# Transposing the normalised tile of a second MoE layer by VectorE and DRAM, in place of TensorE

## The chip, the cores and the metric

One core of a Trainium2 chip runs the whole program. The metric is the device time of one execution in microseconds (us). Engines: TensorE (PE; its weight loads are listed as PEld), VectorE (DVE), ScalarE (ACT), GpSimd (POOL) and SyncE (SP), whose queue issues most DMAs.

## What is computed

A Nystrom attention feeds two MoE layers. The change touches the second one, for 2304 tokens x, model width 512 and inner width 1024:

```python
def _moe2_ref(x, w_in, w_out, g_ln):
    h = x @ w_in
    e = np.exp(h - np.max(h, axis=-1, keepdims=True))
    sm = e / (np.sum(e, axis=-1, keepdims=True) + 1e-09)
    solu = h * sm
    mu = np.mean(solu, axis=-1, keepdims=True)
    var = np.mean((solu - mu) ** 2, axis=-1, keepdims=True)
    ln = (solu - mu) / np.sqrt(var + 1e-06) * g_ln
    return ln @ w_out
```

## The kernel before

The second layer is worked off in 18 tiles of 128 tokens, numbered 0 to 17, in the loop at L1001, after the first layer's last units. Numbers are split into a high half (copied into type fp32r by ACT) and a low half (the rest, subtracted by DVE), and a product takes three matmuls for each pair: high x high, high x low, low x high. In the traces the shapes say f32 for both.

One tile t passes these functions:

- `load_y` (L802) fetches the first layer's output from DRAM (yd) over SP's queue, `split_y` (L812) makes its halves (L127 on ACT, L128 on DVE).
- `gemm3` (L919), the first product: 24 matmuls of 512 columns into a PSUM tile h of two banks. There are two such tiles, so first product t waits until tile t-2's h has been read for the last time, by L940.
- `solu` (L930): the reduce to the row maximum (L935), the exponential (L937, ACT), the multiplication e * h (L940), the sum of squares (L943, ACT), an inverse square root by four Newton steps in short instructions (L953, L955) and the normalisation (L956), which writes a tile s of 128 tokens x 1024. It is a chain that goes from DVE to ACT and back twice.
- `lnT` (L959): the second product needs the 1024 inner columns on the partitions. TensorE transposes s in 8 blocks of 128 x 128 (L967) into two PSUM banks; ACT copies each bank into lh (L970), and DVE subtracts it into ll (L971).
- `gemm4` (L974), the second product: 24 matmuls of 512 columns, a copy out of PSUM by ACT (L983) and a store over SP's queue (L984).

The loop body at t calls, in this order, load_y(t+2), gemm3(t), solu(t), split_y(t+2), gemm4(t-3) and lnT(t-1). lh and ll have three buffers each, s and most others two. First product 0 runs before the loop, among the first layer's last matmuls.

Each engine and each DMA queue works its instructions off in a fixed order. A scheduler sets that order when the program is compiled: it goes by the order of the program text, but where an engine would stand in its own estimate it takes a later instruction that is ready. So an instruction of one tile can stand among those of another. The lines of the first layer that are mentioned: L612 and L623 (matmuls; L623 is the line of every product of three, named h or po by what it writes), L671 (the first layer's second product), L678 (its store to yd by ACT's queue), L222 and L231 (halves of weights), L468 (a transpose by DVE in blocks of 32 x 32).

Of the kernel before, what the change touches and what calls it, by code (L numbers as in the profile page):

```python
# [9 lines left out]
F32 = mybir.dt.float32  # L10
# [4 lines left out]
AF = mybir.ActivationFunctionType  # L15
ALU = mybir.AluOpType
# [6 lines left out]
def f(ap):  # L23
    return ap.bitcast(F32)
# [3 lines left out]
def nystrom_moe_kernel(  # L28
# [13 lines left out]
    V, A, PE, G, SP = nc.vector, nc.scalar, nc.tensor, nc.gpsimd, nc.sync  # L42
# [4 lines left out]
    P = 128  # L47
    L = 32
    R = S // L
    HG = 4  # L50
# [9 lines left out]
    NF2 = F2 // P  # L60
# [3 lines left out]
    NTT = NT // P  # L64
# [3 lines left out]
    PS = bass.MemoryType.PSUM  # L68

    const = ctx.enter_context(tc.tile_pool(name="const", bufs=1))  # L70
    dram = ctx.enter_context(tc.tile_pool(name="dram", bufs=1, space=bass.MemoryType.DRAM))
    yd = dram.tile([P, KD, NT], F32, name="yd")
    yp = dram.tile([P, KD, N], F32, name="yp")

    ident = const.tile([P, P], F32, name="ident")
    mask4 = const.tile([P, HG], F32, name="mask4")
# [603 lines left out]
    with ExitStack():  # L680
# [49 lines left out]
        for g in range(NG):  # L730
            prep, e, c, t, a = attn(0, g)
# [70 lines left out]
        def load_y(t):  # L802
            y = (tr if p2 is None else p2).tile([P, KD, P], F32, tag="y", name="y", bufs=1 if p2 is None else 2)
            SP.dma_start(out=y, in_=yd[:, :, t * P:(t + 1) * P])
            yt[t] = y
            n = min(N - t * P, P)
            if n > 0:
                z = tr.tile([P, KD, P], F32, tag="yz", name="yz")[:, :, 0:n]
                SP.dma_start(out=z, in_=yp[:, :, t * P:t * P + n])
                V.tensor_tensor(out=y[:, :, 0:n], in0=y[:, :, 0:n], in1=z, op=ALU.add)  # L810

        def split_y(t):  # L812
            src = yt[t]
            if t < 2:
                y2 = tr.tile([P, 2, KD, P], F32R, tag="yb", name="yb", bufs=2)
            else:
                y2 = p2.tile([P, 2, KD, P], F32R, tag="yb", name="yb")
            yh, yl = y2[:, 0], y2[:, 1]
            split(yh, yl, src)
            yt[t] = (yh, yl)  # L820
# [4 lines left out]
        for u, (s_, i) in enumerate(units):  # L825
            x = segs[s_][0] * CR // R, i // 4
# [21 lines left out]
        for p in range(U // 2):  # L848
            u = 2 * p + 1
            s_, i = units[u]  # L850
            c, i0, i1 = segs[s_]
# [65 lines left out]
        h2, ln, lt = {}, {}, {}  # L917

        def gemm3(t):  # L919
            yh, yl = yt.pop(t)  # L920
            h = ps_h2[t % len(ps_h2)].tile([P, 2, 512], F32, tag="h2", name="h2")
            for n in range(2):
                pairs = []
                for kk in range(KD):
                    vh, vl = (vi[n, kk // 2][:, kk % 2, x] for x in range(2))
                    pairs += [(yh[:, kk], vh), (yh[:, kk], vl), (yl[:, kk], vh)]
                mm3(h[:, n], pairs)
            h2[t] = h.rearrange("p a b -> p (a b)")
# [29 lines left out]

        def lnT(t):  # L959
            s = ln.pop(t)  # L960
            lh = p2.tile([P, NF2, P], F32R, tag="lh", name="lh", bufs=3)
            ll = p2.tile([P, NF2, P], F32R, tag="ll", name="ll", bufs=3)
            for j in range(2):
                pt = ps_t.tile([P, 512], F32, tag=f"t{j}", name="pt")
                for i in range(4):
                    c = 4 * j + i
                    PE.transpose(pt[:, i * P:(i + 1) * P], s[:, c * P:(c + 1) * P], ident)  # L967
                o = slice(4 * j, 4 * j + 4)
                ptv = pt.rearrange("p (c n) -> p c n", c=4)
                A.activation(out=lh[:, o], in_=ptv, func=AF.Copy)  # L970
                V.tensor_tensor(out=ll[:, o], in0=ptv, in1=f(lh[:, o]), op=ALU.subtract)  # L971
            lt[t] = (lh, ll)

        def gemm4(t):  # L974
            lh, ll = lt.pop(t)
            po = ps_o.tile([P, DM], F32, tag="o", name="po")
            pairs = []
            for c in range(NF2):
                vh, vl = (vo[c // 2][:, c % 2, x] for x in range(2))
                pairs += [(lh[:, c], vh), (lh[:, c], vl), (ll[:, c], vh)]  # L980
            mm3(po, pairs)
            ob = p2.tile([P, DM], F32, tag="ob", name="ob")
            A.activation(out=ob, in_=po, func=AF.Copy)  # L983
            SP.dma_start(out=out[t * P:(t + 1) * P, :], in_=ob)  # L984
# [10 lines left out]
        mo.close()  # L995
        p2 = ctx.enter_context(tc.tile_pool(name="p2", bufs=2, side="right"))
        ps_h2.append(ctx.enter_context(tc.tile_pool(name="ps_h2b", bufs=1, space=PS)))
        ps_t = ctx.enter_context(tc.tile_pool(name="ps_t", bufs=1, space=PS))
        ps_o = ctx.enter_context(tc.tile_pool(name="ps_o", bufs=2, space=PS))
        L4 = 3  # L1000
        for t in range(NTT + L4):  # L1001
            if t + 2 < NTT:
                load_y(t + 2)
            if t < NTT:
                if t:
                    gemm3(t)
                solu(t)
            if t + 2 < NTT:
                split_y(t + 2)
            for _ in range(3 if t < L4 else 100):  # L1010
                if w2 and next(w2[0], "end") == "end":
                    w2.pop(0)
            if t >= L4:
                gemm4(t - L4)
            if 1 <= t <= NTT:
                lnT(t - 1)


def _laid_out(name, a):
# [45 lines left out]
```

## Time and profile before

| | us |
|---|---|
| median of 3 runs | 663.92 |
| lowest and highest | 663.75, 666.64 |
| span of the profiled execution, first to last instruction | 663.1 |
| last matmul's end to the end of the span | 4.1 |
| PE busy | 629.6 (95%) |
| DVE busy | 386.2 (58%) |
| ACT busy | 313.6 (47%) |

For the profiled execution the record has the span; no time beside it is given. Busy shares are over the whole span, of which the second layer's stage takes the last third; rows of that stage, and of the chain of waits that ended last, say more about the change than the shares. A bracket behind a timeline row is the time that the engine was idle before the instruction, and what ended it. [...]

### The profile page before, as it was taken

What the parts mean: (1) busy time and instruction counts of PE and PEld (TensorE: products, weight loads), DVE (VectorE), ACT (ScalarE), POOL (GpSimd) and SP (SyncE); (2) the same over time, 40 slices, a digit from 0 to 9 for tenths busy, and PEclk for the clock granted to TensorE, in tenths of its full rate; (3) what the DMA queues carried; (4) which work ended last, traced back from release to release, by engine and by line L of the source; (5) the groups of instructions that cost most, each with busy time, mean ns of one, the idle gap of its engine ahead of it and who ended that gap; (6) DMA issues with size and microseconds to landing.
All of it is one profiled execution on the core that took longest, in us unless ns stands there. A gap on an engine that the chain in (4) does not pass through costs nothing.

```text
span 663.1 us, 11837 instructions
## 1 busy us (share of the span) xinstructions
PE 629.6 (95%) x4808; PEld 532.7 (80%) x4808; DVE 386.2 (58%) x976; ACT 313.6 (47%) x580; POOL 40.5 (6%) x21
## 2 busy tenths in 40 slices
PE   5688999999999999999997999999999999999997
PEld 2356877889889878898866998997888888888886
DVE  6899898932737235413537613456866666566560
ACT  2379985543637345434644524535534333343431
POOL 3420000000000000000014201310000000000000
PEclk9758899999999999999997999999999999999999
DMA  8998031310212010101055104223101111110001
GB/s 327 400 408 310 0 111 35 109 37 15 95 37 81 29 37 1 38 1 37 1 164 160 37 1 126 102 64 99 48 33 53 44 48 47 36 60 17 17 32 49
DMA packets 30583, 55.43 MB, mean 84 GB/s; under 512 B 3648, under 2 KB 19008, under 8 KB 30528
## 3 DMA queue, kind: packets, MB, share of 16 engines
q1 hardware_dynamic: 25344, 49.36, 21.3%
q10 hardware_dynamic: 5184, 5.31, 2.4%
q8 instruction: 38, 0.62, 0.4%
q14 instruction: 17, 0.14, 0.1%
HBM read 44.63 MB, written 10.03 MB: 82 GB/s over the span
## 4 chain that ended last, share of the span: by engine, by line
PE 87%; ACT 4%; DMA 3%; DVE 2%; issue 1%; POOL 1%; SPq 0%; ACTq 0%; POOLq 0%
PE y L671 30%; PE h L623 28%; PE po L623 15%; PE pa L612 3%; PE pt L967 2%; PE pa L298 2%; DMA r<-in_moe_w_in_dram 2%; PE pa L442 2%; PE pa L429 1%; PE pa L353 1%; POOL r L151 1%; DMA yd<-ye 1%; DMA scr_w<-in_k_dram 1%; DVE r L163 1%; PE pa L410 1%
## 5 line engine op out<-in xcount | busy, mean ns | idle before, releaser
L671 PE MATMUL y<-gh,hl 128*128 128x288 f32 x1024 | 161.7, 304 | 3.7 <-ACT ye L677 2.5
L671 PEld LDWEIGHTS y<-gh,hl 128*128 128x128 f32 x1024 | 144.5, 193 | 15.4 <-issue 7.4
L623 PE MATMUL h<-AT,u 128*128 128x288 f32 x768 | 124.7, 308 | 4.6 <-ACT s L648 2.2
L658 DVE TENSOR_TENSOR gl<-s,gh 128x288 fp32r<-128x288 f32 x128 | 55.0, 467 | 115.5 <-ACT gh L656 60.1
L623 PEld LDWEIGHTS h<-AT,u 128*128 128x128 f32 x768 | 109.8, 195 | 15.1 <-ACT u L615 4.2
L623 PE MATMUL h<-hl,yb 128*128 128x512 f32 x432 | 103.5, 394 | 1.3 <-DVE st L936 0.9
L623 PEld LDWEIGHTS h<-hl,yb 128*128 128x128 f32 x432 | 79.7, 188 | 18.0 <-DVE st L936 1.3
L623 PE MATMUL po<-hl,lh 128*128 128x512 f32 x288 | 88.8, 390 | 0.0
L671 PE MATMUL y<-gl,hl 128*128 128x288 f32 x512 | 83.2, 299 | 0.0
L656 ACT ACTIVATE gh<-s 128x288 fp32r<-128x288 f32 x128 | 50.7, 438 | 56.4 <-PE y L671 56.2
L671 PEld LDWEIGHTS y<-gl,hl 128*128 128x128 f32 x512 | 72.9, 190 | 4.2 <-issue 3.0
L648 ACT ACTIVATE s<-h 128x576 f32<-128x576 f32 x64 | 41.7, 651 | 69.5 <-PE h L623 66.0
L623 PEld LDWEIGHTS po<-hl,lh 128*128 128x128 f32 x288 | 53.9, 188 | 11.1
L623 PE MATMUL po<-hl,ll 128*128 128x512 f32 x144 | 56.1, 390 | 0.0
L151 POOL TENSOR_SCALAR r<-r 128x1024 f32<-128x1024 f32 x10 | 30.5, 3053 | 368.8 <-DMA r<-in_moe_w_in_dram 309.2
L943 ACT ACTIVATE e<-s,st 128x1024 f32<-128x1024 f32 x18 | 20.7, 1151 | 30.0 <-DVE st L942 29.8
L937 ACT ACTIVATE e<-h,st 128x1024 f32<-128x1024 f32 x18 | 20.1, 1117 | 31.2 <-DVE st L936 31.2
L935 DVE TENSOR_REDUCE st<-h 128x1 f32<-128x1024 f32 x18 | 22.0, 1223 | 20.1 <-PE h L623 15.2
L127 ACT ACTIVATE yb<-y 128x512 fp32r<-128x512 f32 x18 | 11.3, 631 | 46.6 <-PE h L623 45.7
L612 PE MATMUL pa<-w,W 64*32 64x512 f32 x256 | 28.1, 642 | 5.1 <-DVE u L616 4.0
L623 PEld LDWEIGHTS po<-hl,ll 128*128 128x128 f32 x144 | 27.0, 188 | 5.6
L616 DVE TENSOR_TENSOR u<-pa,u 128x512 fp32r<-128x512 f32 x32 | 21.1, 687 | 13.9 <-ACT u L615 13.5
(168 smaller groups left out, 678.0 us busy)
## 6 DMA issues: line engine op xcount, KB each, us to landing
r<-in_moe_w_in_dram SPq DMA_DIRECT2D x8, 1024.0 KB, 8.6
ro<-in_moe_w_out_dram SPq DMA_DIRECT2D x8, 1024.0 KB, 17.9
yd<-ye ACTq DMA_DIRECT2D x32, 144.0 KB, 1.8
y<-yd SPq DMA_DIRECT2D x18, 256.0 KB, 3.2
out_dram<-ob SPq DMA_DIRECT2D x18, 256.0 KB, 2.0
w<-in_moe_w_in_dram SPq DMA_DIRECT2D x4, 1024.0 KB, 10.5
v<-in_v_dram SPq DMA_DIRECT2D x8, 512.0 KB, 4.2
r<-in_moe_w_out_dram SPq DMA_DIRECT2D x4, 1024.0 KB, 4.9
```

The lines of the kernel that those rows point to most:

```text
L151: G.tensor_scalar(out=x, in0=x, scalar1=2.0 ** -112, scalar2=None, op0=ALU.mult)
L298: PE.matmul(out[r], lhsT=lhsT[r], rhs=rhs[r], start=True, stop=True)
L612: mm = PE.matmul(po[g][h * L:(h + 1) * L], lhsT=wb[b][r, g, h * L:(h + 1) * L], rhs=w[r, h], start=True, stop=True)
L616: V.tensor_tensor(out=u[:, 1, g], in0=po[g], in1=f(u[:, 0, g]), op=ALU.subtract))
L623: PE.matmul(o, lhsT=a, rhs=b_, start=i == 0, stop=i == n - 1)
L648: A.activation(out=s, in_=h, func=AF.Mish)
L656: A.activation(out=gh[:, e], in_=s[:, e], func=AF.Copy)
L658: V.tensor_tensor(out=gl[:, e], in0=s[:, e], in1=f(gh[:, e]), op=ALU.subtract)
L671: PE.matmul(yb[s_][d][:, 0:N], lhsT=w_out(s, i + e)[:, d * P:(d + 1) * P], rhs=r[:, e], start=i == i0 and e == k == 0, stop=i + 2 == i1 an ...
L935: V.tensor_reduce(out=st[:, 0:1], in_=h, op=ALU.max, axis=AX.X)
L937: A.activation(out=e, in_=h, func=AF.Exp, bias=st[:, 1:2], accum_out=st[:, 2:3])
L943: A.activation(out=e, in_=s, func=AF.Square, bias=st[:, 4:5], accum_out=st[:, 5:6])
```

## The change

`lnT` transposes s on DVE in blocks of 32 x 32, in one instruction for the tile, into a tile sT in SBUF. Four DMAs, one for each block of 32 partitions, write sT to one of three DRAM buffers (lnd), each with 1 KB runs; one DMA reads the buffer back, with the blocks where a full transposition has them, into lT in SBUF. All five are on SP's queue, and the read waits for the writes. A new function `split_ln` makes lh and ll out of lT, with one copy on ACT and one subtract on DVE, both over 1024 columns in SBUF; it is called one round of the loop later than the halves were made before, and still a round ahead of the second product. The two PSUM banks of `ps_t` are no longer used.

```diff
--- before.py
+++ after.py
@@ -71,6 +71,7 @@
     dram = ctx.enter_context(tc.tile_pool(name="dram", bufs=1, space=bass.MemoryType.DRAM))
     yd = dram.tile([P, KD, NT], F32, name="yd")
     yp = dram.tile([P, KD, N], F32, name="yp")
+    lnd = [dram.tile([HG, HG, L, NF2 * L], F32, name=f"lnd{i}") for i in range(3)]
 
     ident = const.tile([P, P], F32, name="ident")
     mask4 = const.tile([P, HG], F32, name="mask4")
@@ -958,17 +959,23 @@
 
         def lnT(t):
             s = ln.pop(t)
+            sT = p2.tile([P, HG, NF2, L], F32, tag="sT", name="sT")
+            V.transpose(out=sT, in_=s.rearrange("p (c q j) -> p q c j", q=HG, j=L))
+            z = lnd[t % len(lnd)]
+            for a in range(HG):
+                SP.dma_start(out=z[a].rearrange("q j x -> j q x"),
+                             in_=sT[a * L:(a + 1) * L].rearrange("j q c i -> j q (c i)"))
+            lT = p2.tile([P, HG, NF2, L], F32, tag="lT", name="lT")
+            SP.dma_start(out=lT.rearrange("p a c i -> p a (c i)"), in_=z.rearrange("a q j x -> (q j) a x"))
+            lt[t] = lT
+
+        def split_ln(t):
+            src = lt[t].rearrange("p a c i -> p c a i")
             lh = p2.tile([P, NF2, P], F32R, tag="lh", name="lh", bufs=3)
             ll = p2.tile([P, NF2, P], F32R, tag="ll", name="ll", bufs=3)
-            for j in range(2):
-                pt = ps_t.tile([P, 512], F32, tag=f"t{j}", name="pt")
-                for i in range(4):
-                    c = 4 * j + i
-                    PE.transpose(pt[:, i * P:(i + 1) * P], s[:, c * P:(c + 1) * P], ident)
-                o = slice(4 * j, 4 * j + 4)
-                ptv = pt.rearrange("p (c n) -> p c n", c=4)
-                A.activation(out=lh[:, o], in_=ptv, func=AF.Copy)
-                V.tensor_tensor(out=ll[:, o], in0=ptv, in1=f(lh[:, o]), op=ALU.subtract)
+            lhv, llv = (x.rearrange("p c (a i) -> p c a i", a=HG) for x in (lh, ll))
+            A.activation(out=lhv, in_=src, func=AF.Copy)
+            V.tensor_tensor(out=llv, in0=src, in1=f(lhv), op=ALU.subtract)
             lt[t] = (lh, ll)
 
         def gemm4(t):
@@ -995,7 +1002,6 @@
         mo.close()
         p2 = ctx.enter_context(tc.tile_pool(name="p2", bufs=2, side="right"))
         ps_h2.append(ctx.enter_context(tc.tile_pool(name="ps_h2b", bufs=1, space=PS)))
-        ps_t = ctx.enter_context(tc.tile_pool(name="ps_t", bufs=1, space=PS))
         ps_o = ctx.enter_context(tc.tile_pool(name="ps_o", bufs=2, space=PS))
         L4 = 3
         for t in range(NTT + L4):
@@ -1014,6 +1020,8 @@
                 gemm4(t - L4)
             if 1 <= t <= NTT:
                 lnT(t - 1)
+            if 2 <= t <= NTT + 1:
+                split_ln(t - 2)
 
 
 def _laid_out(name, a):
```

## Rows read from the trace of the kernel before

**Rows 1.** chain of waits from 400 us, by line; pieces: start, us, what

```profile
by line: PE h L623 38.7%; PE po L623 37.3%; PE y L671 11.1%; PE pt L967 6.1%; DMA yd<-ye 2.0%; issue 0.8%; ACT ye L677 0.5%; ACT hl L225 0.5%; DVE s L940 0.5%; DVE st L935 0.4%; ACT s L648 0.2%; ACT ob L983 0.2%; ACT gh L656 0.2%; DVE y L81
...
462.67 1.06 PE pt L967 x8
...
468.75 0.89 PE pt L967 x8
...
470.34 5.46 PE po L623 x24
...
558.46 0.87 PE pt L967 x8
564.79 5.44 PE po L623 x24
...
648.08 10.91 PE po L623 x48
```

**Rows 2.** busy us by stretch: PE, PEld, DVE, ACT, POOL; PEclk, DMA, GB/s

```profile
553.02:564.79 11.77, 11.77 (x57) 9.83 (x57) 7.52 (x23) 4.54 (x8) 0.00 (x0) 1.00 0.13 45
...
455.67:478.90 23.23, 21.97 (x106) 17.61 (x107) 20.63 (x71) 13.15 (x24) 0.00 (x0) 1.00 0.21 64
```

**Rows 3.** timeline of DVE, one tile: start, us, instruction, [idle before <- releaser]

```profile
567.99 0.15 DVE L938 TENSOR_SCALAR st<-st 128x1 f32<-128x1 f32 x1 [1.27 <-ACT e L937]
...
571.23 0.15 DVE L944 TENSOR_SCALAR st<-st 128x1 f32<-128x1 f32 x1 [1.37 <-ACT e L943]
...
576.60 1.22 DVE L935 TENSOR_REDUCE st<-h 128x1 f32<-128x1024 f32 x1 [1.19 <-PE h L623]
```

**Rows 4.** groups by line and shape: busy us, mean ns | idle before

```profile
L971 DVE TENSOR_TENSOR ll<-pt,lh 128x512 fp32r<-128x512 f32 x36 | 24.3, 684 | 2.7 <-ACT lh L970 2.7
...
L231 DVE TENSOR_TENSOR hl<-dc,hl 128x1024 fp32r<-128x1024 f32 x8 | 10.2, 1270 | 0.1
...
L468 DVE STREAM_TRANSPOSE ATr<-Aw 128x576 f32<-128x576 f32 x6 | 4.6, 772 | 0.2 <-PE pa L411 0.2
...
L222 ACT ACTIVATE hl<-dc 128x1024 fp32r<-128x1024 f32 x8 | 8.5, 1064 | 2.5 <-DVE dc L172 2.1 <-DVE st L388 0.4
```

**Rows 5.** timeline of DVE at the start of the stage

```profile
461.76 0.81 DVE L956 TENSOR_SCALAR s<-s,st 128x1024 f32<-128x1024 f32 x1
...
467.61 0.81 DVE L956 TENSOR_SCALAR s<-s,st 128x1024 f32<-128x1024 f32 x1
468.72 0.15 DVE L938 TENSOR_SCALAR st<-st 128x1 f32<-128x1 f32 x1 [0.29 <-ACT e L937]
...
469.11 1.28 DVE L940 SCALAR_TENSOR_TENSOR s<-e,st,h 128x1024 f32<-128x1024 f32 x1
...
471.57 1.22 DVE L935 TENSOR_REDUCE st<-h 128x1 f32<-128x1024 f32 x1
```

**Rows 6.** instructions on tile yd: duration ns min/median/max, first and last start

```profile
L678 ACTq DMA_DIRECT2D yd<-ye x4: 326/392/445, 450.1 to 454.7; - x4
```

**Rows 7.** DMA issues of the page: KB each, median us from issue to landing

```profile
yd<-ye ACTq DMA_DIRECT2D x32, 144.0 KB, 1.8
y<-yd SPq DMA_DIRECT2D x18, 256.0 KB, 3.2
...
v<-in_v_dram SPq DMA_DIRECT2D x8, 512.0 KB, 4.2
```

**Rows 8.** timeline of DVE at the end, tile 17

```profile
635.47 1.22 DVE L935 TENSOR_REDUCE st<-h 128x1 f32<-128x1024 f32 x1 [1.61 <-PE h L623]
...
644.81 0.81 DVE L956 TENSOR_SCALAR s<-s,st 128x1024 f32<-128x1024 f32 x1
```

**Rows 9.** timeline of PE, then stretches of 1 us as in rows 2

```profile
350.57 1.65 PE L612 MATMUL pa<-w,W 64*32 64x512 f32 x8 [3.97 <-DVE u L616]
...
351.00:352.00 1.00, 1.00 (x8) 0.00 (x0) 1.00 (x2) 0.00 (x0) 0.51 (x1) 0.50 0.00 0
...
357.00:358.00 1.00, 1.00 (x11) 0.42 (x17) 0.41 (x2) 0.02 (x1) 0.00 (x0) 0.63 0.35 81
```

## Prediction

> **What bounds the kernel now.** I read the chain of waits first, because it says whose work the end hangs on. Over the last 263.1 us it gives TensorE nearly everything: the first product of the second layer (L623 h), the second (L623 po), the end of the first layer (L671), and 6.1% to the transposes at L967 [rows 1]. The reader is to see a fixed beat there: 0.87 us of transposes, 5.46 us (564.79 - 558.46 - 0.87) for tile t's first product, 5.44 us for tile t-3's second, 11.77 us a tile, with no pause between the pieces. The busy time in one such stretch says the same: PE 11.77 of 11.77 us, VectorE (DVE) 7.52, ScalarE (ACT) 4.54, DMA 13% [rows 2]. So in this stage what comes off TensorE comes off the time, as long as nothing else becomes slower than 10.90 us a tile.
>
> The second view is DVE's own order in one tile [rows 3]. DVE is a third idle, but in three pieces: 1.27 us waiting for the exponential, 1.37 us for the square, 1.19 us for the next h. Only the last is slack. The other two lie inside a chain that, run alone, takes 11.77 - 1.19 = 10.58 us.
>
> **The change, part by part.** *Removed from TensorE:* 18 blocks of 8 transposes. The chain's 6.1% of 263.1 us is 16.0 us. This is the whole gain.
>
> *ACT and DVE per tile.* Two L971 subtracts of 684 ns go (1.37 us). A transpose of 1024 columns comes: 772 ns for 576 columns [rows 4] scales to 1.37 us if all of it is per column, and 1024-column instructions here take 1.22 to 1.27 us; I take 1.3. One subtract of 1024 columns out of SBUF comes, 1.27 us in its nearest row; I take 1.25. DVE gains 1.2 us, so 7.52 becomes 8.7 of 10.90 us. ACT's two copies become one of about 1.06 us [rows 4]: nothing, beside 4.54 of 10.90. Is 8.7 of 10.9 reachable, with the two waits inside the chain? At the start of the stage it was: for 23 us DVE was busy 20.63 of 23.23 us, 89% [rows 2], because the program's order puts another tile's work in a wait: L956 of tile 1 runs at 467.61, inside tile 2's wait for its exponential, of which 0.29 us is left [rows 5]. That tells me the added work can go into waits when it is ready, and it is ready: tile t-1's normalised rows are finished before tile t's reduce. I take 10.90 us a tile for the steady part.
>
> *The trip through DRAM.* Five more DMAs a tile on SP's queue. The nearest issues are 0.39 us each [rows 6]; four follow each other, so the last starts 1.2 us after the first and lands 1.8 us later (144 KB row); the read of 512 KB then takes 3.2 us (256 KB row) to 4.2 us (512 KB row) [rows 7]. I take 7.2 us with the hand-overs; the ends are 6.2 us and, if each write waited for the one before, 4 x 1.8 + 4.2 = 11.4 us. In the steady part this is hidden: tile t is transposed just after its normalisation, about when first product t+1 ends, and its second product starts behind first product t+3, 21.8 us later, of which transpose, trip, copy and subtract take 10.8. That cover is gone at the two ends. What queues behind the read's wait on SP is the next y load and the output store; both have most of a period to spare, so I cost them at nothing, and if the cover were gone the y load would hold L128 and with it the next first product. Bandwidth is no issue: 1 MB more per 10.9 us is some 96 GB/s on top of 45 [rows 2].
>
> [...]
>
> *Start of the stage.* There the second products are what TensorE has to do while DVE works through tiles 0 to 3. Tile 0 is normalised at 461.76 + 0.81 = 462.57 [rows 5]; with 1.3 + 7.2 + 1.06 + 1.25 us its halves are ready at 473.4, where now its second product starts at 470.34 [rows 1]. Without the two blocks of transposes (1.06 and 0.89 us) first product 3 ends at 468.4. First product 4 needs the h buffer that L940 of tile 2 frees, now at 469.11 + 1.28 = 470.39; two transposes in front of it, less two old subtracts and the 0.29 us of idle time, make it 471.3. So TensorE stands still for 2.9 us. The ends are 0 (an order that finds it work) and 5.0 (if second product 0 stays first in TensorE's queue).
>
> *End of the stage.* Tile 17's reduce starts at 635.47 and its normalisation ends at 645.62, 10.15 us later [rows 8]. Adding 1.3, 7.2, 1.06 and 1.25 its low half is there 20.95 us after first product 17. TensorE then has second products 14, 15 and 16, 3 x 5.45 = 16.4 us, and two matmuls (0.45) that need the high half alone: it loses 4.1 us. The ends are 3.1 and 8.3, from the two ends of the trip.
>
> [...]
>
> **The sum:** -16.0 + 2.9 + 1.6 + 4.1 + 3.2 = -4.2 us. The profiled span of 663.1 us becomes 658.9. The median of the three runs is 663.92, 0.8 us above the span, so the time is 659.7 us.
>
> **The rivals.** *Gaps that close.* The order may give TensorE work at the start, and the clock may hold. Then only the 4.1 us at the end remain: -11.9, 652.0 us. For it: the order is made afresh. [...]
>
> *DVE becomes the bound (slower).* In the steady part each of the two waits is left open in every tile [rows 3]; if they stay so, the chain is 10.58 - 1.37 + 1.3 + 1.25 = 11.76 us a tile instead of 10.90. From tile 3's reduce at 471.57, 0.9 us later, 14 such tiles end at 637.1; the last tile needs 10.15 + 10.8 - 0.45 + 5.46 + 3.2 us, and 4.1 us (663.1 - 658.99) [rows 1] pass behind the last matmul: 670.4, a time of 671 us. It decides as soon as more than 0.3 us a tile of the 2.55 us lies outside the waits; slower than before from 11.44 us a tile. For it: L971 now sits among the short instructions and not in a wait. Against it: rows 5. [...]
>
> *The tile lands late.* Order on each engine is fixed beforehand. If copy and subtract are queued where the tile has not landed, ACT and DVE stand, with the next tile's exponential behind them. With one wait filled the chain has 10.90 - (10.58 - 1.37 + 1.25) = 0.44 us to spare; a stall of 0.8 us a tile costs 14 x 0.4 = 5.6 us more: 665 us.
>
> **How the numbers follow.** A difference under 0.5% (3.3 us) is about what a measurement of this kernel cannot tell from none; faster means under 660.6, slower over 667.2. The forecast has 0.60, and its own range is 654 to 664: 0.37 faster, 0.23 the same. Gaps that close: 0.15, faster. DVE the bound: 0.14, slower but for 0.02. Tile lands late: 0.11, 0.07 the same, 0.04 slower. Together 0.52, 0.32 and 0.16. The range, 651 to 670, takes in the forecast's bounds, the closed gaps and part of the DVE case.
>
> **What would show it.** Right: 10.9 us from reduce to reduce between tiles 5 and 16, no L967, DVE near 8.7 us of that; in TensorE's idle list one pause of some 3 us near 470 and one of 3 to 4 us ahead of the last second product, with the clock at 0.5 behind it. Wrong: a period over 11.3 us with TensorE waiting for L940 (DVE bound), or copy and subtract waiting for a DMA in the steady part (late tile), or no pause at the ends.

## The result, and the profile after

The changed kernel takes 671.36 us (median of 4 runs, 670.27 to 672.48) against 663.84 us for the kernel before on the same chip: 1.0109 of its time, 95% interval 1.0084 to 1.0133. It is **slower by 1.1%**, where the prediction had 659.7 us, and 671.36 lies 1.4 us outside its range. The profiled execution has a span of 670.2 us. Line numbers below are those of the changed kernel: L936 is the reduction, L937 the negated maximum, L938 the exponential, L941 the weighting, L944 the square, L957 the normalisation, L963 VectorE's transposition, L966 the four writes, L969 the read, L977 the copy to `lh`, L978 the subtract to `ll`, L990 and L991 the output copy and store.

The stage is best split at two reductions, those of tile 6 and of tile 17. The forecast's column comes from its own terms: 33.3 us for the end (10.15 + 10.8 - 0.45 + 5.46, then 3.2 for the clock and the 4.1 that pass behind the last matmul), eleven periods of 10.90 us, and what is left of 658.9 for the start.

| stretch | before | forecast | after |
|---|---|---|---|
| start of the span to tile 6's reduction | 505.96 | 505.7 | 509.77 |
| tile 6's to tile 17's reduction (11 tiles) | 129.51 | 119.9 | 124.87 |
| tile 17's reduction to the end | 27.6 | 33.3 | 35.6 |
| span | 663.1 | 658.9 | 670.2 |

All three stretches came out longer than forecast: by 4.1, 5.0 and 2.3 us, together 11.3 of the 11.7 that the time is off; the rest lies in the step from span to time.

**The start.** Timeline of DVE in the changed kernel (start us, us, instruction, [idle before <- releaser]), the first two reductions, one row for both:

```profile
442.70 1.41 DVE L235 SCALAR_TENSOR_TENSOR hl<-cc,gt,hl 128x512 fp32r<-128x512 f32 x2 [0.87 <-ACT hl L226]
454.33 2.36 DVE L936 TENSOR_REDUCE st<-h 128x1 f32<-128x1024 f32 x2 [10.21 <-DMA yd<-ye]
```

Before, the first reduction started at 450.03, released by TensorE. Now it waits for the DMA that writes the first layer's result out of `ye`, which it doesn't read. TensorE pays for it, and then for the clock. Timeline of PE at its long pause, then the busy time around it (columns as in [rows 2]):

```profile
460.01 10.28 PE L624 MATMUL h<-hl,yb 128*128 128x512 f32 x33 [5.22 <-ACT e L938]
```

```profile
455.00:465.00 10.00, 4.99 (x12) 3.96 (x13) 8.76 (x35) 6.45 (x11) 0.00 (x0) 0.68 0.36 106
```

The granted clock of 0.68 in these 10 us (PEclk: the TensorE clock that was granted, as a share of its full speed) is 0.86 in the first five and 0.50 in the rest, from 460 to 465 us. Before it was 1.00 in all of them. Two more pauses that the kernel before doesn't have come in second product 1: 0.51 us for `lh` (491.27) and 1.43 us for `ll` (493.44). Its read had been issued at 483.02, and a read takes 4.3 us; what is late is the copy (490.17, behind a square and an output copy on ACT) and the subtract (492.16, behind a reduction on DVE).

**The steady part.** Two tiles by busy time, then the next two on DVE's timeline, where DVE is busy for as long (17.29 of 22.36 us; the views are those of [rows 2, 3]):

```profile
555.15:577.51 22.36, 21.99 (x97) 17.90 (x96) 17.28 (x48) 9.03 (x14) 0.00 (x0) 1.00 0.49 144
```

```profile
577.51 1.22 DVE L936 TENSOR_REDUCE st<-h 128x1 f32<-128x1024 f32 x1
...
579.31 1.23 DVE L963 STREAM_TRANSPOSE sT<-s 128x1024 f32<-128x1024 f32 x1
...
582.25 1.22 DVE L978 TENSOR_TENSOR ll<-lT,lh 128x1024 fp32r<-128x1024 f32 x1
...
584.90 0.16 DVE L945 TENSOR_SCALAR st<-st 128x1 f32<-128x1 f32 x1 [1.37 <-ACT e L944]
...
588.18 1.25 DVE L963 STREAM_TRANSPOSE sT<-s 128x1024 f32<-128x1024 f32 x1
589.35 1.18 DVE L936 TENSOR_REDUCE st<-h 128x1 f32<-128x1024 f32 x1
...
592.46 0.15 DVE L939 TENSOR_SCALAR st<-st 128x1 f32<-128x1 f32 x1 [1.27 <-ACT e L938]
...
595.70 0.15 DVE L945 TENSOR_SCALAR st<-st 128x1 f32<-128x1 f32 x1 [1.37 <-ACT e L944]
...
596.91 1.22 DVE L978 TENSOR_TENSOR ll<-lT,lh 128x1024 fp32r<-128x1024 f32 x1
...
599.86 1.22 DVE L936 TENSOR_REDUCE st<-h 128x1 f32<-128x1024 f32 x1
```

No L936 has an idle time in front of it: the 1.19 us of slack in [rows 3] is gone, and from tile 6's reduction on DVE never waits for TensorE. It is busy 17.28 of 22.36 us, 8.64 a tile (forecast 8.7), but of the four waits of two tiles only one, the exponential's at 579.31, has a transposition in it. The other transposition stands right before a reduction (588.18), one subtract right behind the weighting (582.25), where it delays the square, and one among the short instructions (596.91). Reductions alternate between 10.52 and 11.84 us; three longer ones (11.92, 12.36 and 12.42) bring the mean of eleven to 11.35. In the last two of these a transposition stands between the reduction and L937, so the exponential too starts later.

TensorE itself hardly loses its beat: between 500 and 634 us it waits 0.9 us in all, for `ll`. DVE falls behind it instead. First product 17 on PE's timeline:

```profile
625.70 5.60 PE L624 MATMUL h<-hl,yb 128*128 128x512 f32 x24
```

It ends at 631.30, and its reduction starts at 634.64, 3.3 us later. In the kernel before a reduction follows its first product at once ([rows 8]: released by TensorE). The lag lengthens the way to the end.

**The end.** Pauses of PE after tile 17's reduction at 634.64:

```profile
638.31 0.73 PE L624 MATMUL po<-hl,lh 128*128 128x512 f32 x2 [1.56 <-ACT lh L977]
640.21 0.80 PE L624 MATMUL po<-hl,ll 128*128 128x512 f32 x1 [1.17 <-DVE st L943]
...
649.98 0.73 PE L624 MATMUL po<-hl,lh 128*128 128x512 f32 x2 [1.63 <-ACT lh L977]
651.24 0.50 PE L624 MATMUL po<-hl,ll 128*128 128x512 f32 x1 [0.53 <-DVE ll L978]
...
658.40 0.73 PE L624 MATMUL po<-hl,lh 128*128 128x512 f32 x2 [1.88 <-ACT lh L977]
659.66 0.57 PE L624 MATMUL po<-hl,ll 128*128 128x512 f32 x1 [0.53 <-DVE ll L978]
```

Three second products, 15, 16 and 17, are late, each with two pauses (7.3 us together); the forecast had one pause of 4.1. Twice the clock falls to 0.50 behind them (busy time of two stretches, PEclk is the first number after POOL):

```profile
643.00:646.00 3.00, 3.00 (x9) 2.32 (x8) 2.79 (x7) 0.00 (x0) 0.00 (x0) 0.50 0.53 157
...
660.00:663.00 3.00, 3.00 (x8) 2.31 (x7) 0.00 (x0) 0.00 (x0) 0.00 (x0) 0.50 0.00 0
```

What is late is read from the two queues, SP's DMA issues and ACT's timeline:

```profile
634.74 1.27 SPq L966 DMA_DIRECT2D lnd<-sT  x3
638.77 0.36 SPq L991 DMA_DIRECT2D out_dram<-ob  x1
639.17 0.43 SPq L966 DMA_DIRECT2D lnd<-sT  x1
641.60 0.38 SPq L969 DMA_DIRECT2D lT<-lnd  x1
649.01 0.36 SPq L991 DMA_DIRECT2D out_dram<-ob  x1
649.47 1.86 SPq L966 DMA_DIRECT2D lnd<-sT  x4
653.46 0.38 SPq L969 DMA_DIRECT2D lT<-lnd  x1
```

```profile
648.38 0.60 ACT L990 ACTIVATE ob<-po 128x512 f32<-128x512 f32 x1 [6.83 <-PE po L624]
648.88 1.05 ACT L977 ACTIVATE lh<-lT 128x1024 fp32r<-128x1024 f32 x1
656.61 0.60 ACT L990 ACTIVATE ob<-po 128x512 f32<-128x512 f32 x1 [6.68 <-issue]
657.29 1.06 ACT L977 ACTIVATE lh<-lT 128x1024 fp32r<-128x1024 f32 x1
```

Tile 16's fourth write stands behind an output store from 636.01, when the third is out, to 639.17; tile 17's four writes, whose data L963 had ready at 646.10 (it started at 644.85 and took 1.25), were issued at 649.47, right behind the store of tile 15. On ACT the copy of tile 16 stands behind the output copy of tile 15, which waits for TensorE until 648.38. Tile 16's read had been issued at 641.60 and took 3.8 us, so its data lay ready 3.5 us before the copy. On SP's queue the store of tile 15 waits for 7.0 us, from 641.98 to 649.01, and the writes behind it, whose data is ready from 646.10, are issued 3.4 us late.

The trip itself is near its forecast. DMA issues of the page (KB each, median us from issue to landing):

```profile
lnd<-sT SPq DMA_DIRECT2D x72, 128.0 KB, 2.4
lT<-lnd SPq DMA_DIRECT2D x18, 512.0 KB, 4.3
```

For tile 17 it is 7.8 us from the first issue (649.47) to the copy that it released (657.29), against 7.2.

### The profile page after: what moved, and what is told of

Its sections match the earlier page's. It is cut to its first block, busy times and chain, and to the rows that moved or that the text cites. A ratio compares the mean times of both kernels' runs of the same rounds, so it can differ in the third digit from the quotient of the medians.

```text
span 670.2 us, 11692 instructions
## 1 busy us (share of the span) xinstructions
PE 620.8 (93%) x4664; PEld 518.6 (77%) x4664; DVE 404.9 (60%) x976; ACT 313.3 (47%) x562; POOL 41.3 (6%) x21
## 4 chain that ended last, share of the span: by engine, by line
PE 59%; DVE 15%; issue 8%; ACT 8%; DMA 8%; POOL 1%; SPq 1%; ACTq 0%; DVEq 0%; POOLq 0%
PE y L672 28%; PE h L624 17%; PE po L624 4%; PE pa L613 3%; DVE st L936 2%; DVE ll L978 2%; DMA r<-in_moe_w_in_dram 2%; PE pa L299 2%; DMA lT<-lnd 2%; DVE st L954 1%; DMA lnd<-sT 1%; PE pa L443 1%; ACT e L944 1%; PE pa L430 1%; DVE st L956 1%
## 5 line engine op out<-in xcount | busy, mean ns | idle before, releaser
L672 PE MATMUL y<-gh,hl 128*128 128x288 f32 x1024 | 159.8, 302 | 4.0 <-ACT ye L678 2.6
L672 PEld LDWEIGHTS y<-gh,hl 128*128 128x128 f32 x1024 | 142.4, 190 | 16.5 <-issue 7.6
L624 PE MATMUL h<-AT,u 128*128 128x288 f32 x768 | 124.7, 308 | 3.7 <-ACT s L649 1.8
L624 PEld LDWEIGHTS h<-AT,u 128*128 128x128 f32 x768 | 109.4, 194 | 14.9 <-ACT u L616 4.7
L624 PE MATMUL h<-hl,yb 128*128 128x512 f32 x432 | 104.2, 397 | 5.6 <-ACT e L938 5.2
L624 PEld LDWEIGHTS h<-hl,yb 128*128 128x128 f32 x432 | 82.6, 192 | 24.1 <-issue 6.6
L624 PE MATMUL po<-hl,lh 128*128 128x512 f32 x288 | 92.5, 403 | 5.6 <-ACT lh L977 5.6
L624 PEld LDWEIGHTS po<-hl,lh 128*128 128x128 f32 x288 | 55.8, 195 | 18.9 <-ACT lh L977 7.3
L624 PE MATMUL po<-hl,ll 128*128 128x512 f32 x144 | 58.8, 409 | 4.6 <-DVE ll L978 3.4
L152 POOL TENSOR_SCALAR r<-r 128x1024 f32<-128x1024 f32 x10 | 31.5, 3146 | 366.7 <-DMA r<-in_moe_w_in_dram 303.5
L938 ACT ACTIVATE e<-h,st 128x1024 f32<-128x1024 f32 x18 | 20.1, 1114 | 57.2 <-DVE st L937 57.2
L624 PEld LDWEIGHTS po<-hl,ll 128*128 128x128 f32 x144 | 28.1, 195 | 13.9 <-DVE ll L978 6.2
L944 ACT ACTIVATE e<-s,st 128x1024 f32<-128x1024 f32 x18 | 20.7, 1152 | 24.7 <-DVE st L943 23.4
L978 DVE TENSOR_TENSOR ll<-lT,lh 128x1024 fp32r<-128x1024 f32 x18 | 21.9, 1219 | 12.1 <-ACT lh L977 12.1
L936 DVE TENSOR_REDUCE st<-h 128x1 f32<-128x1024 f32 x18 | 21.7, 1208 | 12.1 <-DMA yd<-ye 10.2
```

Source lines behind the costliest of these rows:

```text
L152: G.tensor_scalar(out=x, in0=x, scalar1=2.0 ** -112, scalar2=None, op0=ALU.mult)
L624: PE.matmul(o, lhsT=a, rhs=b_, start=i == 0, stop=i == n - 1)
L672: PE.matmul(yb[s_][d][:, 0:N], lhsT=w_out(s, i + e)[:, d * P:(d + 1) * P], rhs=r[:, e], start=i == i0 and e == k == 0, stop=i + 2 == i1 an ...
L936: V.tensor_reduce(out=st[:, 0:1], in_=h, op=ALU.max, axis=AX.X)
L938: A.activation(out=e, in_=h, func=AF.Exp, bias=st[:, 1:2], accum_out=st[:, 2:3])
L944: A.activation(out=e, in_=s, func=AF.Square, bias=st[:, 4:5], accum_out=st[:, 5:6])
```

## The experiments

Four theories of the loss, one for each stretch and one against them all. **Start**: the pool `p2` grew by `sT` and `lT`, so tiles of the second layer lie where `ye` lay, and must wait until it is written out. **Steady part**: DVE's order leaves waits open. **End**: transfers and copies stand in queues behind output stores and copies. **Rival**: it is the trip through DRAM as such. Times are medians, and each ratio is to the kernel before on the same chip; the table gives the reductions of the profiled execution. Profiled executions differ by some us before the second layer begins (its first reduction starts at 445.38 us in run 6 and at 449.34 in run 7), so a single span is compared by its stretches.

| run | tile 6 | period | tile 17 to end | span | median us | ratio to before, 95% interval |
|---|---|---|---|---|---|---|
| before | 505.96 | 11.77 | 27.6 | 663.1 | 663.84 | 1 |
| after | 509.77 | 11.35 | 35.6 | 670.2 | 671.36 | 1.0109 (1.0084 to 1.0133) |
| order fixed | 510.99 | 10.88 | 37.5 | 668.2 | 669.34 | 1.0076 (1.0059 to 1.0092) |
| store on GpSimd's queue | 507.89 | 10.95 | 34.5 | 662.8 | 665.93 | 1.0027 (1.0012 to 1.0042) |
| own pool | 503.91 | 11.36 | 35.7 | 664.5 | 662.77 | 0.9987 (0.9961 to 1.0013) |
| no trip | 508.08 | 11.19 | 23.1 | 654.3 | 655.47 | 0.9867 (0.9852 to 0.9882) |
| store moved, output copy behind | 506.92 | 11.04 | 31.5 | 659.9 | 662.16 | 0.9978 (0.9958 to 0.9998) |
| all three edits | 499.12 | 10.88 | 34.2 | 653.0 | 657.90 | 0.9914 (0.9881 to 0.9946) |
| and tiles 16, 17 by TensorE | 503.01 | 10.88 | 28.4 | 651.1 | 652.60 | 0.9835 (0.9805 to 0.9866) |
| and tile 0 by TensorE | 502.65 | 10.84 | 28.4 | 650.3 | 652.13 | 0.9839 (0.9815 to 0.9862) |
| the same without tile 0, store on SP | 503.15 | 10.95 | 27.3 | 650.9 | 653.19 | 0.9830 (0.9813 to 0.9846) |
| before, store on GpSimd's queue | 505.45 | 11.77 | 28.7 | 663.6 | 665.46 | 1.0016 (1.0005 to 1.0028) |

**1. DVE's order fixed.** The transposition of a tile is put behind the next tile's L937, so that it always runs in the wait for the exponential.

```
+ mark[t] = V.tensor_scalar(out=st[:, 1:2], in0=st[:, 0:1], scalar1=-1.0, ...)
...
+ with tc.issue_after(mark[t + 1].ins) if t + 1 in mark else nullcontext():
      V.transpose(out=sT, in_=s.rearrange("p (c q j) -> p q c j", q=HG, j=L))
```

> Edit: the transpose of tile t-1 is queued behind the short instruction after tile t's reduce, so that in every tile it falls into the wait for the exponential; no work is added or left out. If DVE's chain is what bounds the steady part (it alternates 10.52 and 11.84 us, 11.18 on average, and the long ones are those with the transpose ahead of the reduce), the period goes to TensorE's 10.90 us and some 11 tiles give back 3 us: 668 us. If the steady part is bound by the trip through DRAM or by its traffic, the order on DVE changes less than 1 us: 671.

Measured: 669.34 us. One tile in the steady part by busy time, and DVE's timeline there:

```profile
554.51:565.39 10.88, 10.88 (x49) 9.01 (x48) 8.79 (x24) 4.63 (x8) 0.00 (x0) 1.00 0.51 147
```

```profile
554.51 1.23 DVE L936 TENSOR_REDUCE st<-h 128x1 f32<-128x1024 f32 x1 [0.23 <-PE h L624]
...
556.31 1.24 DVE L964 STREAM_TRANSPOSE sT<-s 128x1024 f32<-128x1024 f32 x1
...
560.90 0.15 DVE L945 TENSOR_SCALAR st<-st 128x1 f32<-128x1 f32 x1 [1.37 <-ACT e L944]
```

The period is 10.88 us, TensorE is busy all of it, and the reduction waits for TensorE again. So the 11.35 of the changed kernel is the order's doing, with the same work on every engine. The time fell by 2.0 us, where 3 were expected. In the profiled execution tile 17 starts 4.0 us sooner (630.67 against 634.64), though tile 6 is 1.2 later, and the end gives back 1.9: TensorE comes sooner to products whose halves aren't there, and its longest pause there is 5.42 us.

**2. Output store on GpSimd's queue.**

```
- SP.dma_start(out=out[t * P:(t + 1) * P, :], in_=ob)
+ G.dma_start(out=out[t * P:(t + 1) * P, :], in_=ob)
```

> Edit: the output stores go to GpSimd's queue instead of SP's. If the last tile's writes stand behind an output store on SP's queue (tile 17 is transposed at 646.1 us, its first write starts at 649.5, right behind the store of tile 15), they start at once and the end comes some 3 us earlier: 668 us. If the trip is late for its own length, under 1 us.

Measured: 665.93 us, 5.4 less than the changed kernel, but not where expected: the end fell by 1.1 us only, the period from 11.35 to 10.95. Tile 17's writes are now issued at 639.82, as soon as its transposition ends, so SP's queue is out of the way; the copies of `lh` still stand behind output copies on ACT. The period fell because the order is planned afresh: each tile's subtract now stands in the wait for the exponential. DVE's timeline of one tile there:

```profile
541.20 1.19 DVE L936 TENSOR_REDUCE st<-h 128x1 f32<-128x1024 f32 x1
...
542.96 1.22 DVE L978 TENSOR_TENSOR ll<-lT,lh 128x1024 fp32r<-128x1024 f32 x1
...
549.98 0.81 DVE L957 TENSOR_SCALAR s<-s,st 128x1024 f32<-128x1024 f32 x1
550.82 1.25 DVE L963 STREAM_TRANSPOSE sT<-s 128x1024 f32<-128x1024 f32 x1
```

An edit of a queue moved the order of another engine, and the run therefore doesn't isolate the queue.

**3. An own pool for the two new tiles**, so that the other tiles of the second layer lie at their old addresses.

```
- sT = p2.tile([P, HG, NF2, L], F32, tag="sT", name="sT")
+ sT = p3.tile([P, HG, NF2, L], F32, tag="sT", name="sT")
...
+ p3 = ctx.enter_context(tc.tile_pool(name="p3", bufs=2, side="right"))
```

(`lT` likewise.)

> Edit: the two new SBUF tiles get a pool of their own, opened behind the old one, so that the old tiles lie where they lay before the change. If the first reduce waits for the first layer's last stores only because its small tile of statistics now lies where the stored tile lay, it starts some 4 to 5 us earlier and the time falls by 3 to 5 us: 667 us. If the start is lost to the trip through DRAM, the gain is under 1 us.

Measured: 662.77 us, 8.6 less than the changed kernel, where 3 to 5 were expected. The first reduction is released by TensorE again:

```profile
449.96 1.23 DVE L936 TENSOR_REDUCE st<-h 128x1 f32<-128x1024 f32 x1 [5.00 <-PE y L672]
```

Tile 6 starts 5.9 us sooner, at 503.91, and the granted clock in 455 to 465 is 1.00 again. Period (11.36) and end (35.7) are untouched. So the late start comes from where the tiles lie, and 5.9 of the 8.6 us are shown to be its price; the rest is open. That the first reduction waits because one of the old tiles had moved onto `ye`, and which one, is inferred, not shown. The runs of this kernel reach from 658.51 to 666.36 with mean clocks from 0.981 to 0.959; in the profiled one, at the slow end of them, the clock in 345 to 365 us is 0.74 where all others but run 1 (0.74) have 0.83 or 0.84, ahead of the code that was changed.

**4. No trip.** The four writes and the read are left out and the halves are made from `sT`: the exchange of the 32x32 blocks between partitions is left out. `sT` gets four buffers, so that the pool keeps its size.

```
- sT = p2.tile([P, HG, NF2, L], F32, tag="sT", name="sT")
+ sT = p2.tile([P, HG, NF2, L], F32, tag="sT", name="sT", bufs=4)
...
- z = lnd[t % len(lnd)]
- for a in range(HG):
-     SP.dma_start(out=z[a]..., in_=sT[...]...)
- lT = p2.tile(...)
- SP.dma_start(out=lT..., in_=z...)
- lt[t] = lT
+ lt[t] = sT
```

> Edit: the four writes and the read are left out, and the halves are made of the block-transposed tile in SBUF (so the second product is taken of other numbers); DVE and ACT do the same work. If the trip costs at the two ends alone and DVE bounds the steady part, the steady period stays near 11.2 us and the stretch from the last reduce to the end falls from 35.6 to about 25 us: 661 us. If the trip or its traffic also bounds the steady part, the period falls to 10.90 us as well: 657 us or less.

Measured: 655.47 us, under the 661 of the first theory and within the 657 of the second; the period decides between them. It is 11.19 without a single transfer, so the steady part was not bound by the trip: 0.16 us a tile at most can be its share, and DVE's order, planned afresh here too, remains the bound (its reductions wait for TensorE once, 0.3 us). The first reduction is late as before (455.26, behind the same DMA). The end is 23.1 us instead of 35.6: trip, queues and clock together cost 12.5 us there. At the end the rival has most of it.

**5. The store on GpSimd's queue, and on ACT the output copy behind the next tile's `lh` copy.** Against run 2:

```
- A.activation(out=lhv, in_=src, func=AF.Copy)
+ cut[t] = A.activation(out=lhv, in_=src, func=AF.Copy)
...
+ with tc.issue_after(cut[t + 1].ins) if t + 1 in cut else nullcontext():
      A.activation(out=ob, in_=po, func=AF.Copy)
...
+ if 2 <= t <= NTT + 1:
+     split_ln(t - 2)
  if t >= L4:
      gemm4(t - L4)
```

(and the old call of `split_ln` behind `lnT` goes)

> The output stores leave SP's queue for GpSimd's, and on ScalarE the copy of a finished output tile is issued behind the lh copy of the next tile, so that no lh copy stands behind an output copy. Theory of the two queues (the end of the changed kernel is longer than forecast because tile 17's writes stand behind tile 15's store on SP and lh of tiles 16 and 17 stand behind the output copies on ScalarE): from tile 17's reduction to the end 31 to 33 us, against 34.5 with the store moved alone and 35.6 in the changed kernel; about 663.5 us in all. Rival (the end is the bare round trip of the last two tiles and the low clock after the pauses, no queue in it): the end stays at 34.5 or more, 666 us.

Measured: 662.16 us, end 31.5, as the theory of the two queues had it. ACT near tile 16's copy, in run 2 and then in this one:

```profile
638.44 0.60 ACT L990 ACTIVATE ob<-po 128x512 f32<-128x512 f32 x1 [3.20 <-PE po L624]
638.94 1.05 ACT L977 ACTIVATE lh<-lT 128x1024 fp32r<-128x1024 f32 x1
```

```profile
636.37 1.06 ACT L978 ACTIVATE lh<-lT 128x1024 fp32r<-128x1024 f32 x1 [1.07 <-DMA lT<-lnd]
637.48 0.60 ACT L992 ACTIVATE ob<-po 128x512 f32<-128x512 f32 x1
```

The copy now follows its transfer, 2.6 us sooner, and of the two falls of the clock one is left (in 650 to 655 us it is 1.00, in run 2 0.66). The two queues explain 35.6 - 31.5 = 4.1 us of the end, the fall of the clock that went with them included. The rest of the way to 27.6 is the trip: three pauses, 4.0 us together with the longest at 2.79, and one fall of the clock, which is what the prediction had (4.1 and one fall).

**6. All three edits together** (own pool, order fixed, store on GpSimd's queue; `split_ln` ahead of `gemm4` as in run 5, without the order of the copies).

> Own pool for the two new tiles, VectorE's order fixed behind the next tile's reduction, output stores on GpSimd's queue: three edits that each answer to one of the three causes. If the causes are independent, tile 6's reduction starts at 503.9 (as with the own pool alone), the steady period is 10.9 (as with the order alone), tile 17's reduction starts at 624, the end is 34 to 36 us, and the time some 660 us (-11 against the changed kernel). Rival (what is gained before the end is lost in it, since the tail then waits for the trip and the clock): tile 17 at 624 but the end 40 us or more, 666 us.

Measured: 657.90 us, 13.5 less than the changed kernel; period 10.88, end 34.2. By stretches the gains add: from the first reduction to tile 6 it takes 53.74 us (own pool 53.95, changed kernel 55.44), the period is that of run 1, and the end is near that of run 2. The profiled execution is the fastest of its four, and its first reduction (445.38) comes some 4 us sooner than in the next run (449.34), before any of this; so tile 6 at 499.12 is no better than there.

**7. The last two tiles by TensorE**, as in the kernel before, all others as in run 6.

```
+ def by_pe(t):
+     return t < 0 or t >= NTT - 2
...
  s = ln.pop(t)
+ if by_pe(t):
...                            # the block of the kernel before, with `ps_t` opened again
+     return
...
  def split_ln(t):
+     if by_pe(t):
+         return
```

> As the run with all three edits, and the last two tiles, 16 and 17, are transposed by TensorE as in the kernel before, so the end has no round trip. Theory (the trip belongs in the steady part only, where TensorE's time is the bound; at the end it is latency and pauses): end 27 to 29 us as in the kernel before (27.6), time 651 to 654 us, faster than both kernels by 10 us or more. Rival (the end is long because of the pause before the last products and the low clock that follows, whoever transposes): end 33 us or more, 658 us or more.

Measured: **652.60 us, 0.9835 of the kernel before**. By busy time, one steady tile and then the stretch from tile 17's reduction to the last matmuls; the chain of waits from 400 us by line:

```profile
557.41:568.29 10.88, 10.88 (x49) 9.01 (x48) 8.70 (x24) 4.63 (x8) 0.54 (x1) 1.00 0.47 145
...
622.69:646.00 23.31, 23.31 (x112) 19.28 (x110) 9.34 (x25) 7.04 (x12) 1.62 (x3) 1.00 0.11 39
```

```profile
by line: PE po L624 34.6%; PE h L624 33.0%; PE y L672 9.4%; issue 5.9%; DMA r<-in_moe_w_out_dram 2.0%; DVE s L941 1.9%; DMA yd<-ye 1.3%; POOL r L152 1.2%; DVE st L954 1.0%; DVE st L936 0.9%; DVE st L956 0.7%; DVE s L957 0.6%; DVE sT L981 0.
```

TensorE doesn't pause behind tile 6, the clock is 1.00 from tile 17's reduction to the last matmuls (622.69 to 646.00 us), and the chain is TensorE's, as in [rows 1] but without the transposes. In the changed kernel the same chain was `issue` 16.9%, L624 h 10.1% and po 9.6%. Against the kernel before the gain adds up: 11 x 0.89 in the steady part, 2.3 at the start (from the first reduction to tile 6's 53.67 us instead of 55.93), less 0.8 at the end, 11.3 us; measured 11.1.

At the start TensorE has these pauses in this run:

```profile
456.89 10.72 PE L624 MATMUL h<-hl,yb 128*128 128x512 f32 x46 [0.89 <-DVE st L937]
469.08 5.73 PE L624 MATMUL h<-hl,yb 128*128 128x512 f32 x24 [1.47 <-DVE s L941]
475.31 2.78 PE L624 MATMUL h<-hl,yb 128*128 128x512 f32 x11 [0.51 <-DVE st L956]
```

Together 2.9 us, and none for `lh` or `ll`. But the kernel before has a pause of 0.9 us behind the same instruction (L936 there), so what is new is 1.47 + 0.51 = 2.0 us. The 1.47 us stand in front of first product 4, which waits until L941 has read tile 2's h: the very pause that the prediction described and put at 2.9 us. The clock stays at 1.00 from 455 to 475 us.

**8. Tile 0 by TensorE too** (`t < 1` for `t < 0` in `by_pe`).

> As the run before it (last two tiles by TensorE) with tile 0 by TensorE too, so that the first round trip, during which TensorE has only one other product to do, is gone. Forecast of the prediction's start term: a pause of about 2.9 us at the first use of a fetched tile goes, so 2 to 3 us less than the run before it, 649 to 651 us. Rival (the pause at the start is VectorE's chain over the first tiles and not the trip): no difference, within 1 us.

Measured: 652.13 us; the interval covers run 7's, so the time is the rival's. Its reason isn't. TensorE's waits from 440 to 512 us (us in total, times, longest):

```profile
PE h L624 <- DVE st L937: 0.9, 1, 0.9
PE po L624 <- DVE ll L998: 0.4, 2, 0.2
PE h L624 <- ACT yb L128: 0.4, 1, 0.4
```

The pauses of 1.47 and 0.51 us are gone, since second product 0 now stands there (from 467.97), so they did come from the first trip. But TensorE pays 1.09 us for the transposition and waits 0.4 us for `ll`; the 0.5 us that are left can't be told from none.

**9. Run 7 with the store back on SP's queue.**

> The fastest version with its output stores back on SP's queue (own pool, VectorE's order fixed, tiles 16 and 17 by TensorE). Theory (with the order fixed and no trip in the end, the queue has nothing left to decide: the trips of the steady part have a tile's time to spare): period 10.9, end 28 to 29 us, 652 to 653 us, as with the other queue. Rival (trips behind a store come late in the steady part too): period above 11.1, 655 us or more.

Measured: 653.19 us, period 10.95, end 27.3: as run 7 within the intervals. With the order fixed and no trip in the end the queue makes no difference that can be measured.

**10. A control: the kernel before, with its store on GpSimd's queue.**

> The kernel before, with one edit: the stores of the finished output tiles go over GpSimd's queue, as in the fastest version so far. A control. Theory (the gain of that version comes from the transposition that left TensorE's steady beat, and the queue matters only where a trip to DRAM shares SP's queue): period 11.77, end 27.6, 663.9 us, ratio within 0.997 to 1.003. Rival (the store on SP's queue costs the kernel before as well, and part of the gain is the queue's): 660 us or less.

Measured: 665.46 us, ratio 1.0016. Nothing of run 7's gain is the queue's; the end is 1 us longer with it.

## Why the prediction was wrong

- **Removed from TensorE, 16.0 us: right.** With the order fixed the period is 10.88 us, forecast 10.90. The durations held too: L963 1.24 us (taken 1.3), L978 1.22 (1.25), L977 1.05 (1.06), DVE 8.64 us a tile (8.7). ("1024-column instructions here take 1.22 to 1.27 us" isn't true of all: L956 takes 0.81 and L940 1.28 [rows 5].)
- **"I take 10.90 us a tile for the steady part": the largest failure, 5.0 us by the table.** That the work could go into the waits was read from the start of the stage [rows 5], where two tiles are in flight on DVE; in the steady part the order filled one wait of four. The rival "DVE becomes the bound" had the mechanism and, with all waits open, 11.76 us a tile. Every second tile took that long (11.84); two tiles make 23.52, less the one wait filled (1.2), 22.3, and 22.36 was measured. The condition put beside it was wrong by the prediction's own numbers: without the old subtracts the chain is 10.58 - 1.37 = 9.21 us, its waits included; work put into the waits adds nothing to it and work outside them adds itself, so it is paid for from 10.90 - 9.21 = 1.69 us a tile on, not from 0.3. And 9.21 is too short: in run 2, with the one subtract in a wait, reduction to the end of the normalisation takes 549.98 + 0.81 - 541.20 = 9.59 us, so the two old subtracts had lengthened the chain by 1.0 us and not by 1.37. Then 1.3 us a tile are free; in the changed kernel the work outside the waits took 22.36 / 2 - 9.59 = 1.6. The sign named for this rival, TensorE waiting for L940, did not show: the stretch ended with DVE 3.3 us behind TensorE instead. With the order alone set right (run 1) the period is as forecast, and the end gives part of it back.
- **Start of the stage: 4.1 us, a wait that the sum lacks.** What cost the time is a wait that the diff doesn't show: with two new tiles in the pool its other tiles lie elsewhere, and the first reduction waits for a DMA of the first layer; the 5.22 us pause and the fall of the clock follow from it. Run 3 prices it at 5.9 us. The two terms that the sum has were too high: with the own pool the start is 1.8 us better than forecast (503.91 against 505.7). The pause in front of first product 4 is there in run 7 and gone in run 8, so its mechanism was right, but with the next one it measured 2.0 us in place of 2.9, and the 1.6 us for the clock did not come.
- **End of the stage: 2.3 us.** "What queues behind the read's wait on SP is the next y load and the output store; both have most of a period to spare, so I cost them at nothing" looked at what stands behind the trip, not at what the trip stands behind: tile 17's writes behind a store on SP, tile 16's copy behind an output copy on ACT. Run 5 prices both at 4.1 us. The trip was sized well (7.8 against 7.2 us).
- **The clock: right in kind, wrong in place.** The sum has 1.6 us for a fall at the start and 3.2 for one at the end, 4.8 together. Both terms are the author's estimates, from the one fall of [rows 9] (0.50 behind a pause of 3.97 us); no run shows either. What the runs showed in their place is one fall to 0.50 behind the 5.22 us pause (460 to 465 us) and two at the end (643 to 646 and 660 to 663 us); run 7, with neither the long pause nor those at the end, has none from 450 to 645 us.
- The rival that ended at 671 us has the measured time by coincidence: of its 0.86 us a tile, 0.45 came (5.0 us over eleven), and the other 6.4 us are from places it didn't name. "The tile lands late" did not come: between 500 and 620 us the copies wait 0.5 us in all for a read. The changed kernel, with all 18 tiles by VectorE, is 1.1% slower; with order, pool and queue arranged for it and the last two tiles by TensorE (run 7) the same transposition of the other sixteen comes with a gain of 11.1 us.

## What to carry to other kernels

Work taken from the bounding engine bought its time here once it was queued inside the waits of the engine that got it (10.88 us a tile in run 1, 11.35 in the changed kernel): follow one steady tile in the order that is really issued, not a stretch in which two overlap. The trip through memory cost 0.16 us a tile at most in the steady part and, with its queues and the clock, 12.5 us at the end of the pipeline (run 4); the old, short path for the last two tiles brought the end from 34.2 to 28.4 us (runs 6 and 7). And look for what an edit moves without naming it: addresses in a shared pool (the sign of it here was a wait of 10.21 us for a DMA that the instruction has no data from), and transfers that now share a queue with stores that wait.

## Not expected of the hardware

Behind a pause of 5.22 us the granted clock was 0.50 (460 to 465 us). At the end of the changed kernel it was 0.50 behind the pairs of pauses of 1.56 and 1.17 us (643 to 646) and of 1.88 and 0.53 (660 to 663), but not behind the pair between them, 1.63 and 0.53: in 650 to 655 us the clock was 1.00. Behind three pauses of 0.5 to 1.5 us within 20 us at the start (run 7, 455 to 475 us) it was 1.00 as well. What tells these cases apart was not tried.
